# Row sums of five more blocks turned through a DMA and added on GpSimd; the last three stores on ScalarE's queue; a new order of the work

## The chip, the core and the metric

The kernel runs on one core of a Trainium2 chip. The metric is the device time of one execution in microseconds (us); the kernel before takes 324.15 us, the median of three runs (324.11 to 324.23). The profiled execution, from which all durations below are read, took 324.28 us.

## The reference

Two layers follow each other. An attention block with 32 learned queries pools each batch of 12544 rows, and its result serves as keys and values for the rows themselves; then every row goes through two products, an element-wise maximum and an output product.

```python
def mab(q, kv):                                  # scale = 1 / sqrt(128)
    s = scale * (q @ kv.transpose(0, 2, 1))
    a = np.exp(s - s.max(-1, keepdims=True))
    a /= a.sum(-1, keepdims=True) + 1e-09
    return a @ kv

h = mab(I, x)            # x (4, 12544, 128), I (4, 32, 128): h (4, 32, 128)
y = mab(x, h)            # (4, 12544, 128), taken as 50176 rows
out = np.maximum(y @ w1, y @ w2) @ w_out         # w1, w2 (128, 1024), w_out (1024, 128)
```

## The kernel before, in words

**The algebra.** y is not formed. With e2 = exp(scale x hT), a row's output is linear in e2 up to its denominator d, the sum of its 32 exponentials: out = (relu(e2 hwd) w_out + e2 m1) / d, where hwd = h (w2 - w1) and m1 = h w1 w_out. So a row needs 32 exponentials, a product of inner size 32, a relu, a product with w_out, and a scale by 1/d when the result leaves PSUM.

**Tiles.** A batch is 98 chunks of 128 rows; a block is up to four quarters of up to four chunks each, so that four products of inner size 32 run beside each other in the four row groups of TensorE. There are 28 blocks, 0 to 6 of batch 0, 7 to 13 of batch 1, 14 to 20 of batch 2, 21 to 27 of batch 3; all five that the change names are full, four chunks wide. TensorE works in three modes, and the planner charges for each switch:

- column mode: `stage` (line 637) makes a block's scores, whose exponential ScalarE writes as e2 (line 656); `pool_scores` (341) and `pool_accum` (397) pool the next batch;
- row mode: a `phase` (1093) makes four units of e2 hwd into four of the eight PSUM banks, some of them e2 m1 ("L"), and each unit's relu is taken out of PSUM by ScalarE (1119) or VectorE (1122);
- full mode: `final_one` (907) multiplies a relu chunk with w_out, eight matmuls for a chunk, up to 32 for a group, which is what is stored together. Some 14 of them stand between two phases.

**Denominators.** They are had in two ways. `dens` gives a full-mode matmul of e2 against `ones_q`, 128 by 4, for each chunk (698) and a VectorE reciprocal from PSUM (708), for a block and mostly the next one together. A block that is "turned" (21 to 27 before) does without TensorE: `den_turn` turns its e2 by a DMA transpose on SP's queue (717), `den_sum` adds the 32 columns by five GpSimd instructions (727 once, 729 four times), and `den_rp` takes the reciprocal on VectorE (736). `evict_group` multiplies a finished group by the reciprocal on VectorE (939) and stores it (969), from SP's queue or GpSimd's.

**The order.** All engines' streams are written out by a planner that runs while the program is built. It keeps a clock for TensorE, ScalarE and VectorE (class `Clock`), asks `ready` whether a piece of side work may go, decides between a phase and a final matmul by these times, and departs from its own choice where the table `DEV` says so. SP's queue has the 14 DMA transposes of x for each following batch (172), the transposes of the pooled exponentials (378) and the stores outside GpSimd's ranges; GpSimd has loads of x (166) and the other stores. The loads of a batch wait for the last `pool_accum` of the batch before it, by a copy named `pace` (164).

Of the kernel before, what the change touches and what calls it, by code (L numbers as in the profile page):

```python
# [19 lines left out]
class Clock:  # L20


    PAIR = 0.0558
# [4 lines left out]
    def __init__(self):  # L28
        self.pe = self.act = self.dve = 0.0
        self.mode = "full"  # L30
        self.bank = [0.0] * 8
        self.idle = {}
        self.log = []
        self.busy = {}
# [7 lines left out]
    def run(self, us, mode="full", ready=0.0, why="data"):  # L42
# [7 lines left out]
        return self.pe + self.LAT  # L50

# [17 lines left out]
class Block:  # L69


    def __init__(self, quarters, full=()):
# [4 lines left out]
        self.rp = None  # L77
        self.units = []
# [24 lines left out]
def kernel(  # L103
# [29 lines left out]
    rpp = ctx.enter_context(tc.tile_pool(name="rpp", bufs=5))  # L133
# [34 lines left out]
    def transpose_x_dma(b, j):  # L168
# [6 lines left out]
        st[b]["T", j] = ck.pe  # L175
# [21 lines left out]
    with tc.manual_schedule(engines={ET.PE, ET.DVE, ET.Activation, ET.Pool, ET.SP}):  # L197
# [128 lines left out]
        NEU = 5  # L326
        NU = K // U
# [7 lines left out]
        def pool_scores(b, u):  # L335
# [19 lines left out]
            ck.bank[bi] = ck.on_act(end, 0.65)  # L355
# [20 lines left out]
        def pool_turn(b, u):  # L376
            eT = etp.tile([128, 4, 128], F16, name=f"eT_{b}_{u}", tag="eT", bufs=NEU)
            nc.sync.dma_start_transpose(eT, st[b]["eu", u][0].rearrange("p (j t) -> p j t", j=4))
            st[b]["eT", u] = eT, ck.pe

        def pool_accum(b, u):
# [7 lines left out]
            if last:  # L389
                nc.vector.reduce_sum(out=acc[:, C : C + 1], in_=st[b]["es"], axis=AX.X)  # L390
                ck.on_dve(st[b]["eu", u][1], 0.1)
# [33 lines left out]
            end = ck.run(0.58 if last else 0.49, "col")  # L425
# [8 lines left out]
            if last and b + 1 < B:  # L434
                for i in range(7):
                    load_x(b + 1, i, acc[:, C : C + 1] if i == 0 else None)

# [178 lines left out]

        for n, blk in enumerate(blocks):
            blk.turned = n > 20

        def stage(blk, now=True):  # L620
# [25 lines left out]
            end = ck.run(0.054 * wd, "col")  # L646
# [36 lines left out]
        def dens(blk):  # L683
# [23 lines left out]
            end = ck.run(0.029 * n)  # L707
            nc.vector.reciprocal(out=rp[:, 0:n, :].rearrange("p t q -> p (t q)"), in_=ps[:, 0 : 4 * n])
            ck.bank[bi] = ck.on_dve(end, 0.18 + 0.001 * 4 * n)
            for blk in blks:  # L710
                blk.rpr = ck.dve + 0.2

        def den_turn(blk):
            uid[0] += 1
            eT = etp.tile([128, 4, 128], F16, name=f"den_{uid[0]}", tag="eT", bufs=NEU)[:, 0 : blk.width, :]
            e2 = blk.e2[:, 0 : 128 * blk.width]
            nc.sync.dma_start_transpose(eT, e2.rearrange("p (t k) -> p t k", k=128))
            blk.den = eT, ck.pe
            pending.append((den_sum, (blk,)))

        def den_sum(blk):
            wd = blk.width
            eT = blk.den[0].rearrange("p t (q m) -> p (t q) m", m=M)
            lo = 512 * (blk.index % 2)
# [5 lines left out]
            blk.dsum = acc[:, :, 0], ck.pe  # L730
            pending.append((den_rp, (blk,)))

        def den_rp(blk):
# [3 lines left out]
            ck.on_dve(ck.pe, 0.066 + 0.025 * wd)  # L737
# [187 lines left out]
        def evict_group(g, end):  # L925
# [39 lines left out]
            queue = nc.scalar if g is groups[-1] else nc.gpsimd if by_pool else nc.sync  # L965
            for b, c, s, m in runs:
                h = 2 if m == 4 and not by_pool and (gi in (56, 60, 64, 68, 72, 76) or 78 <= gi < 95) else m
                for lo in range(0, m, h):
                    queue.dma_start(out=outr[b, :, c + lo : c + lo + h, :], in_=osb[:, s + lo : s + lo + h, :])  # L969
# [24 lines left out]
        def want_linear():  # L994
# [113 lines left out]
        def evict_relu(q, a, u, bi, ps, end, eng=None):  # L1108
# [6 lines left out]
            ready = end + 0.03  # L1115
            if eng is None:
                eng = max(ck.act, ready) + 0.477 <= max(ck.dve, ready) + 0.597
            if eng:
                nc.scalar.activation(out=dst, in_=src, func=AF.Relu)  # L1119
                t = ck.on_act(ready, 0.477)  # L1120
            else:
                nc.vector.tensor_scalar(out=dst, in0=src, scalar1=0.0, scalar2=None, op0=ALU.max)  # L1122
                t = ck.on_dve(ready, 0.597)
# [36 lines left out]
        def ready(f, a):  # L1160

            now = ck.pe
            if f is den_turn:
                return a[0].staged <= now
            if f is den_sum:
                return a[0].den[1] + 7.5 <= now
            if f is den_rp:
                return a[0].dsum[1] + 3.0 <= now and a[0].index <= groups[min(state["g"], len(groups) - 1)].blk.index + 1
# [3 lines left out]
            if f is pool_turn and a[1] >= NEU and ("sum", a[1] - NEU) not in d:  # L1172
# [194 lines left out]
```

## Time and profile before

| what | value |
|---|---|
| median of three runs | 324.15 us (324.11 to 324.23) |
| the profiled execution | 324.28 us |
| span of its trace, first to last instruction | 322.5 us |
| TensorE busy, weight loads apart | 316.3 us, 5372 matmuls |
| VectorE busy | 280.9 us, 506 instructions |
| ScalarE busy | 281.6 us, 565 instructions |
| GpSimd busy | 63.2 us, 136 instructions |
| granted TensorE clock, mean | 0.994 |

Of the execution, 1.8 us lie outside the span. Busy time is the union of an engine's instructions. A matmul's recorded time is its latency (220 ns for the 128x128 product), while the next one may start some 56 ns later; so TensorE's pace is read from starts, and its busy share says only whether it had nothing in flight. "PE" is TensorE, "PEld" its weight loads, "DVE" VectorE, "ACT" ScalarE, "POOL" GpSimd; a q behind a name is that engine's DMA issue. Times are from the span's start.

### The profile page before, as it was taken

How to read it: one execution, taken by the hardware profiler on the slowest of the kernel's cores; microseconds unless marked ns; L12 is line 12 of the kernel's file. 1: busy time of each engine (PE TensorE's matmuls, PEld its weight loads, DVE VectorE, ACT ScalarE, POOL GpSimd, SP SyncE). 2: the span in 40 equal slices, each digit the busy share in tenths (PEclk: the TensorE clock that was granted, in tenths of full speed). 3: DMA queues.
4: the chain of work that ended last, by engine and by line, in shares of the span. 5: the costliest groups of instructions: out<-in, count | busy, mean ns of one | idle time of the engine just before them, and what ended most of it. 6: DMA issues, size and time to landing. Idle time of an engine off the chain costs nothing.

```text
span 322.5 us, 12607 instructions
## 1 busy us (share of the span) xinstructions
PE 316.3 (98%) x5372; PEld 241.3 (75%) x5372; DVE 280.9 (87%) x506; ACT 281.6 (87%) x565; POOL 63.2 (20%) x136
## 2 busy tenths in 40 slices
PE   7999999999999999999999999999999999999996
PEld 3976777777777777777777777777777777777786
DVE  3369999899979998898999998989998999899973
ACT  4779899999978999989888999988969999999960
POOL 7472012212040121221040021222006400330000
PEclk9899999999999999999999999999999999999999
DMA  8999999974289999984269999963525322442233
GB/s 206 207 263 213 218 235 233 228 152 102 100 172 241 219 234 230 239 137 128 101 124 239 232 250 226 242 133 117 118 92 109 132 83 88 120 134 95 88 116 116
DMA packets 74072, 54.12 MB, mean 168 GB/s; under 512 B 56064, under 2 KB 64032, under 8 KB 74016
## 3 DMA queue, kind: packets, MB, share of 16 engines
q1 hardware_dynamic: 64320, 27.88, 40.7%
q0 software_dynamic: 9552, 25.37, 33.5%
q8 instruction: 42, 0.69, 0.9%
q14 instruction: 14, 0.11, 0.1%
q10 hardware_dynamic: 144, 0.07, 0.1%
HBM read 27.54 MB, written 25.69 MB: 165 GB/s over the span
## 4 chain that ended last, share of the span: by engine, by line
PE 92%; DMA 5%; ACT 1%; issue 1%; POOL 0%; DVE 0%; POOLq 0%
PE ps L907 62%; PE ps L1093 23%; DMA xn<-in_x_dram 5%; PE ps L637 2%; PE ps L397 2%; PE ps L341 1%; ACT relu L1119 1%; PE ps L698 1%; PE ps L531 0%; PE ps L236 0%; PE ps L315 0%; PE ps L442 0%; PE ps L266 0%; ACT hwd L504 0%; PE ps L489 0%
## 5 line engine op out<-in xcount | busy, mean ns | idle before, releaser
L1119 ACT ACTIVATE relu<-ps 128x512 f16<-128x512 f32 x462 | 244.0, 605 | 23.6 <-PE ps L1093 16.1
L1122 DVE TENSOR_SCALAR relu<-ps 128x512 f16<-128x512 f32 x322 | 206.5, 682 | 17.7 <-PE ps L1093 15.2
L907 PE MATMUL ps<-woutp,relu 128*128 128x128 f16 x3136 | 216.9, 220 | 0.1
L907 PEld LDWEIGHTS <-relu 128*128 128x128 f16 x3136 | 176.7, 98 | 38.7 <-issue 28.2
L1093 PE MATMUL ps<-e,hwd 32*128 32x512 f16 (+2 forms) x888 | 88.9, 358 | 0.6 <-ACT hwd L504 0.6
L969 POOL DMA_DIRECT2D out_dram<-o x44 | 23.8, 542 | 148.3 <-DVE o L939 134.1
L939 DVE TENSOR_TENSOR o<-ps,rp 128x512 f32<-128x512 f32 (+3 forms) x80 | 51.2, 639 | 1.6 <-PE ps L907 1.1
L1093 PEld LDWEIGHTS <-hwd 32*128 32x128 f16 x888 | 24.9, 91 | 22.1 <-issue 0.9
L1093 PE MATMUL ps<-m,e 32*128 32x128 f16 x381 | 38.9, 217 | 0.0
L1093 PEld LDWEIGHTS <-e 32*128 32x128 f16 x381 | 21.3, 92 | 2.9 <-issue 0.4
L939 DVE TENSOR_TENSOR o<-ps,rpt 128x512 f32<-128x512 f32 (+3 forms) x28 | 17.3, 619 | 4.2 <-PE ps L884 2.2
L166 POOL DMA_DIRECT2D xn<-in_x_dram x33 | 17.9, 556 | 6.4 <-DMA xn<-in_x_dram 4.5
L247 DVE COPY xT<-ps 128x768 f16<-128x768 f16 (+6 forms) x11 | 4.8, 459 | 8.7 <-PE ps L236 8.7
L352 ACT ACTIVATE eu<-ps 128x512 f16<-128x512 f32 x18 | 10.8, 616 | 0.0
L236 PE MATMUL ps<-identity,xn 128*128 128x128 f16 x98 | 9.5, 237 | 1.2 <-DVE inducingT L786 0.6
L656 ACT ACTIVATE e<-ps 128x512 f16<-128x512 f32 (+2 forms) x21 | 10.4, 584 | 0.0
L727 POOL TENSOR_TENSOR w1T<-den 128x256 f32<-128x256 f16 (+1 forms) x7 | 4.4, 630 | 26.7 <-DMA den<-e 26.7
L729 POOL TENSOR_TENSOR w1T<-w1T 128x64 f32<-128x64 f32 (+4 forms) x28 | 8.4, 300 | 2.2
L236 PEld LDWEIGHTS <-xn 128*128 128x128 f16 x98 | 6.7, 106 | 2.8 <-DVE xn L748 0.9
L250 ACT COPY xT<-ps 128x768 f16<-128x768 f16 (+5 forms) x10 | 6.4, 670 | 2.1 <-PE ps L236 2.0
L637 PE MATMUL ps<-xT,hT 128*32 128x512 f16 (+3 forms) x118 | 8.3, 355 | 0.0
L637 PEld LDWEIGHTS <-hT 128*32 128x32 f16 x118 | 3.2, 94 | 3.8 <-issue 2.1
(95 smaller groups left out, 115.1 us busy)
## 6 DMA issues: line engine op xcount, KB each, us to landing
out_dram<-o POOLq DMA_DIRECT2D x44, 256.0 KB, 3.8
xn<-in_x_dram POOLq DMA_DIRECT2D x24, 448.0 KB, 9.7
out_dram<-o SPq DMA_DIRECT2D x28, 256.0 KB, 2.7
out_dram<-o SPq DMA_DIRECT2D x46, 128.0 KB, 1.8
wf<-in_moe_w_dram POOLq DMA_DIRECT2D x4, 256.0 KB, 5.9
xn<-in_x_dram POOLq DMA_DIRECT2D x3, 224.0 KB, 8.8
xT<-xn SPq DMA_TRANSPOSE x42, 5.5
xf<-in_x_dram SPq DMA_DIRECT2D x1, 512.0 KB, 3.7
```

The costliest lines, as they stand in the source:

```text
L166: nc.gpsimd.dma_start(out=xn_at[b, i][lo:hi, 0:n, :], in_=xr[b, lo:hi, k0 : k0 + n, :])
L236: nc.tensor.transpose(ps[:, j, :], xn_at[0, i][:, g + j, :], identity16)
L352: nc.scalar.activation(out=eu, in_=ps, func=AF.Exp, scale=scale, accum_out=st[b]["es"][:, u : u + 1])
L637: nc.tensor.matmul(out=ps[32 * q : 32 * (q + 1), 128 * t : 128 * (t + n)], lhsT=hq, rhs=xT[:, c : c + n, :], start=True, stop=True, tile_p ...
L656: nc.scalar.activation(out=blk.e2[:, lo:hi], in_=ps[:, lo:hi], func=AF.Exp, scale=st[0]["rs"] if blk.b == 0 else scale,)
L729: nc.gpsimd.tensor_add(acc[:, :, 0:n], acc[:, :, 0:n], acc[:, :, n : 2 * n])
L907: nc.tensor.matmul(out=g.ps[:, 128 * c : 128 * (c + 1)], lhsT=g.blk.relu[q][:, 128 * (jb * w4 + t) : 128 * (jb * w4 + t + 1)], rhs=woutp[: ...
L939: nc.vector.tensor_mul(osb[:, 0:n, :], g.ps[:, 0 : n * C].rearrange("p (s c) -> p s c", s=n), rp)
L969: queue.dma_start(out=outr[b, :, c + lo : c + lo + h, :], in_=osb[:, s + lo : s + lo + h, :])
L1093: nc.tensor.matmul(**seq[i])
L1119: nc.scalar.activation(out=dst, in_=src, func=AF.Relu)
L1122: nc.vector.tensor_scalar(out=dst, in0=src, scalar1=0.0, scalar2=None, op0=ALU.max)
```

## The change

1. Blocks 5, 10, 11, 12 and 19 join the turned ones: the test `n > 20` becomes membership in `TURNED`. `ready` holds a transpose back while the planner thinks that loads are under way (26.5 us from the issue of a batch's loads), or that SP's queue is far behind; `etp` has six eT buffers instead of five, `rpp` nine reciprocal buffers instead of five.
2. The planner gets clocks for SP and GpSimd, other constants for most steps, and lets `small_m1(0)` go from the second phase on.
3. The last three groups' stores are issued by ScalarE, instead of the last one alone. Which groups of 70 to 94 are stored in two halves changes.
4. `DEV` is a new table (24 entries for 28), so nearly every engine's stream after the first 29 us stands in another order.

```diff
-            blk.turned = n > 20
+        TURNED = (5, 10, 11, 12, 19, 21, 22, 23, 24, 25, 26, 27)
+            blk.turned = n in TURNED
...
+    def on_sp(self, ready, us, slow=0.0):
+        self.sp = max(self.sp, ready)
+        self.sp += slow if slow and self.sp < self.loads else us
+        return self.sp + (8.0 if self.sp < self.loads else 4.0)
...
-        st[b]["T", j] = ck.pe
+        st[b]["T", j] = max(ck.pe, ck.on_sp(ck.pe, 1.75, 4.0) - 7.0)
...
+                ck.loads = ck.pe + 26.5
...
-            blk.den = eT, ck.pe
+            blk.den = eT, ck.on_sp(ck.pe, 1.3)
...
-            lo = 512 * (blk.index % 2)
+            lo = 512 * (turned.index(blk) % 2)
...
-            queue = nc.scalar if g is groups[-1] else nc.gpsimd if by_pool else nc.sync
+            queue = nc.scalar if g in groups[-3:] else nc.gpsimd if by_pool else nc.sync
...
-            ready = end + 0.03
+            ready, ready_v = end - 0.005, end + 0.03
...
-                eng = max(ck.act, ready) + 0.477 <= max(ck.dve, ready) + 0.597
+                eng = max(ck.act, ready) + 0.487 <= max(ck.dve, ready_v) + 0.601
...
             if f is den_turn:
-                return a[0].staged <= now
+                if len(eTs) > NEU and not eTs[-NEU - 1]():
+                    return False
+                n = len(turned)
+                return a[0].staged <= now and ck.loads <= now and ck.sp <= now + (8.0 if a[0].b == 2 else 0.8) and (n < 3 or turned[n - 3].dsum is not None)
             if f is den_sum:
-                return a[0].den[1] + 7.5 <= now
+                n = turned.index(a[0])
+                return a[0].den[1] + 3.0 <= now and ck.pool <= now and (n < 2 or turned[n - 2].rp is not None)
```

Counted over the whole streams, TensorE has 20 matmuls of 128x4 and their 20 weight loads fewer (76 before, 56 now), and every other kind as often as before. TensorE changes between its modes as often as before: 222 stretches of row mode, 25 of column mode, 226 of full mode in both. Relu units move from VectorE to ScalarE, 11 of them; VectorE has two reciprocals from PSUM fewer (11, now 9) and five from SBUF more; SP issues five transposes more, GpSimd 25 additions more.

**First place: TensorE at the denominators of block 5**, whose e2 is e_216 before. The four matmuls with e_216 and two with e_252 (block 6) stand between two groups of final matmuls (ps_2078, then ps_2160):

```order
L698 MATMUL ps_2184<-ones_q,e_216_1572 128x4
L698 LDWEIGHTS e_216_1572
L698 MATMUL ps_2184<-ones_q,e_216_1572 128x4
L698 LDWEIGHTS e_252_1797
L698 MATMUL ps_2184<-ones_q,e_252_1797 128x4
L698 LDWEIGHTS e_252_1797
L698 MATMUL ps_2184<-ones_q,e_252_1797 128x4
L907 LDWEIGHTS relu_1777
L907 MATMUL ps_2160<-woutp,relu_1777 128x128
L907 LDWEIGHTS relu_1777
L907 MATMUL ps_2160<-woutp,relu_1777 128x128
```

Now the final matmuls of block 5's first group (ps_2214; line 907 is line 924 here) follow those of the group before it directly:

```order
L924 LDWEIGHTS relu_1719
L924 MATMUL ps_2030<-woutp,relu_1719 128x128
L924 LDWEIGHTS relu_1719
L924 MATMUL ps_2030<-woutp,relu_1719 128x128
L924 LDWEIGHTS relu_1788
L924 MATMUL ps_2214<-woutp,relu_1788 128x128
L924 LDWEIGHTS relu_1788
L924 MATMUL ps_2214<-woutp,relu_1788 128x128
```

Block 5's matmuls are gone; those of block 6 stand with block 7's, one group later.

**Second place: SP's queue while batch 2 is turned.** xT_94 is the turned x of batch 2, eT_0 to eT_5 its turned pooled exponentials. Before:

```order
L172 DMA_TRANSPOSE xT_94<-xn_87 128x7x128 x2
L172 DMA_TRANSPOSE xT_94<-xn_88 128x7x128 x2
L378 DMA_TRANSPOSE eT_0_3174<-eu_0_3130 128x4x128
L172 DMA_TRANSPOSE xT_94<-xn_89 128x7x128 x2
L172 DMA_TRANSPOSE xT_94<-xn_90 128x7x128
L378 DMA_TRANSPOSE eT_1_3361<-eu_1_3312 128x4x128
L172 DMA_TRANSPOSE xT_94<-xn_90 128x7x128
L378 DMA_TRANSPOSE eT_2_3487<-eu_2_3441 128x4x128
L378 DMA_TRANSPOSE eT_3_3517<-eu_3_3455 128x4x128
L378 DMA_TRANSPOSE eT_4_3802<-eu_4_3764 128x4x128
L378 DMA_TRANSPOSE eT_5_3831<-eu_5_3771 128x4x128
```

Now (line 172 is 179, 378 is 387, 717 is 731; the den tiles are those of blocks 10, 11 and 12):

```order
L179 DMA_TRANSPOSE xT_94<-xn_87 128x7x128 x2
L731 DMA_TRANSPOSE den_3122<-e_332_2341 128x4x128
L179 DMA_TRANSPOSE xT_94<-xn_88 128x7x128 x2
L387 DMA_TRANSPOSE eT_0_3201<-eu_0_3160 128x4x128
L179 DMA_TRANSPOSE xT_94<-xn_89 128x7x128
L387 DMA_TRANSPOSE eT_1_3255<-eu_1_3188 128x4x128
L179 DMA_TRANSPOSE xT_94<-xn_89 128x7x128
L179 DMA_TRANSPOSE xT_94<-xn_90 128x7x128 x2
L731 DMA_TRANSPOSE den_3488<-e_477_3167 128x4x128
L387 DMA_TRANSPOSE eT_2_3510<-eu_2_3467 128x4x128
L387 DMA_TRANSPOSE eT_3_3522<-eu_3_3474 128x4x128
L731 DMA_TRANSPOSE den_3593<-e_479_3174 128x4x128
```

Block 10's transpose stands ahead of the last six of x, those of blocks 11 and 12 behind them, among those of the pooled exponentials.

**Third place: ScalarE's last rows.** Before, four relus and the last store:

```order
L1119 ACTIVATE relu_7754<-ps_8018 128x512
L1119 ACTIVATE relu_7908<-ps_8020 128x512
L1119 ACTIVATE relu_7754<-ps_8051 128x512
L1119 ACTIVATE relu_7908<-ps_8053 128x512
L969 DMA out_dram<-o_8186 128x128
```

Now the last relus and three stores, of which the first two were SP's last two:

```order
L1139 ACTIVATE relu_7847<-ps_8110 128x4x128
L1139 ACTIVATE relu_8018<-ps_8112 128x512
L990 DMA out_dram<-o_8173 128x384
L990 DMA out_dram<-o_8195 128x256
L990 DMA out_dram<-o_8208 128x128
```

49 lines of the change are left out of this document (31 added, 18 removed), and 7 rows, old and new, of the table DEV.

## The prediction

> **What bounds the kernel now.** I read the busy time by stages first, since a mean over the span hides which stage has room. The columns are the stretch, its length, and each engine's busy us with its instructions:
>
> ```profile
> 21.00:29.00 8.00, 7.31 (x103) 4.31 (x101) 7.21 (x17) 7.58 (x18) 4.21 (x7) 1.00 1.22 205
> 29.00:100.00 71.00, 71.00 (x1226) 53.29 (x1223) 64.40 (x114) 65.73 (x134) 10.97 (x21) 1.00 0.89 184
> 100.00:200.00 100.00, 99.98 (x1681) 75.68 (x1679) 92.81 (x162) 91.67 (x185) 15.83 (x30) 1.00 0.95 197
> 200.00:300.00 100.00, 100.00 (x1688) 76.37 (x1685) 92.90 (x163) 91.70 (x182) 18.68 (x48) 1.00 0.47 123
> ```
>
> From 29 us on TensorE has something in flight all the time: 71.00 of 71, 99.98 of 100, 100.00 of 100. VectorE and ScalarE stand at 92 to 93%, with some 8 us of room in 100, and GpSimd is nearly free. Then the list of waits of TensorE alone (us in total, times, longest), of which these are the longest four:
>
> ```profile
> PE ps L753 <- DVE warm L217: 1.2, 1, 1.2
> PE ps L236 <- DVE inducingT L786: 0.6, 1, 0.6
> PE ps L1093 <- ACT hwd L504: 0.6, 1, 0.6
> PE ps L236 <- DVE xn L748: 0.4, 1, 0.4
> ```
>
> All belong to the start, the third at 24.2 us. "In flight" can still hide a small wait, so I looked at the starts where a phase stands between final matmuls, and found this as the worst after 29 us (start, length, line, count):
>
> ```profile
> 84.39 0.50 PE L907 MATMUL ps<-woutp,relu 128*128 128x128 f16 x6
> 84.81 0.51 PE L1093 MATMUL ps<-e,hwd 32*128 32x256 f16 x5
> 85.26 0.51 PE L907 MATMUL ps<-woutp,relu 128*128 128x128 f16 x6
> ...
> 152.62 0.78 PE L907 MATMUL ps<-woutp,relu 128*128 128x128 f16 x11
> 153.33 0.39 PE L1093 MATMUL ps<-e,hwd 32*128 32x512 f16 x4
> 153.65 0.90 PE L907 MATMUL ps<-woutp,relu 128*128 128x128 f16 x13
> ```
>
> At 152.62 eleven final matmuls take 0.78 us with the last one's latency of 0.22, so one starts 0.056 us after another; the last starts at 153.18, and the first after the phase at 153.65: a phase costs 0.47 us. At 84.39 six finals start, the last at 84.67, and the next one at 85.26: 0.59 us, so the phase between them waited for 0.12 us. Reading every phase that way, eight are longer than usual by 0.02 us or more, 0.3 us in all. So **the kernel is bound by what TensorE issues**, and after 29 us only about 0.3 us of its time is waiting. What the change can take away is issue time and these 0.3 us; what it can add is waits.
>
> **The change part by part.** *The matmuls that go.* Here are the ones of two blocks before, with the groups of the same line:
>
> ```profile
> 152.07 0.51 PE L907 MATMUL ps<-woutp,relu 128*128 128x128 f16 x6
> 152.42 0.34 PE L698 MATMUL ps<-ones_q,e 128*128 128x4 f16 x8
> ...
> L698 PE MATMUL ps<-ones_q,e 128*128 128x4 f16 x76 | 3.5, 165 | 0.0
> L698 PEld LDWEIGHTS <-e 128*128 128x128 f16 x76 | 3.1, 96 | 0.2 <-issue 0.2
> ```
>
> Eight start at 152.42 and the next final matmul at 152.62 (row above): 0.20 us, 25 ns each. The group's mean of 165 ns is latency that overlaps, and its weight loads of 96 ns overlap too, since eight of them pass in those 0.20 us. Bounds for one matmul: 25 ns by the starts, 96 ns if the loads came one after another. I take 25, since it is the step that the path shows. 20 x 25 ns = **-0.50 us**. They sit in full mode between final matmuls, so no mode switch goes with them, and by the two streams the numbers of switches, phases, final matmuls and all others are equal: these terms cancel. The stream up to 29 us is the same, so the start's waits stay.
>
> The Trainium skill, page "TensorE: Matmul & The Clock Gate", section "LDWEIGHTS (loading the stationary operand)", prices a load by its columns, at columns/1.2 ns: 107 ns for 128. By that price 20 loads in series would be -2.1 us. The 96 ns of the row agree with the price for one load, and the starts 25 ns apart disagree with its being paid in series.
>
> *What takes their place.* For each of the five blocks a transpose on SP, five additions on GpSimd, a reciprocal on VectorE:
>
> ```profile
> L717 SPq DMA_TRANSPOSE den<-e x7: 1191/1217/1994, 242.5 to 280.0; - x7
> ...
> L727 POOL TENSOR_TENSOR w1T<-den x7: 423/664/667, 245.0 to 283.6; 128x256 f32<-128x256 f16 x6, 128x128 f32<-128x128 f16 x1
> ...
> L729 POOL TENSOR_TENSOR w1T<-w1T x28: 205/248/457, 245.8 to 285.6; 128x64 f32<-128x64 f32 x7, 128x32 f32<-128x32 f32 x7, 128x16 f32<-128x16 f32 x7, 128x128 f32<-128x128 f32 x6
> ...
> L736 DVE RECIPROCAL rpt<-w1T x7: 194/243/245, 253.8 to 305.1; 128x16 f32<-128x16 f32 x6, 128x8 f32<-128x8 f32 x1
> ...
> L708 DVE RECIPROCAL rp<-ps x11: 249/347/349, 28.5 to 240.6; 128x32 f32<-128x32 f32 x7, 128x20 f32<-128x20 f32 x2, 128x16 f32<-128x16 f32 x1, 128x24 f32<-128x24 f32 x1
> ```
>
> SP gets 5 x 1.2 = 6.1 us. GpSimd gets 5 x (0.66 + 4 x 0.3) = 9 us, on an engine that is busy 10.97 us of 71 and 15.83 of 100. VectorE gets 5 x 0.24 and loses 2 x 0.35: +0.5 us. None of it lies on TensorE's path, and the cover is time: between a block's reciprocal and the first product that uses it the stream of VectorE has other groups' products, three for block 5, two, one and four for blocks 10 to 12. If the cover went, VectorE would stand at the reciprocal with its relus behind it, and TensorE for their banks; one turn of such a chain is a transpose's landing plus the sums, some 3.5 + 2.2 us.
>
> *The relus that move.* Eleven units go from VectorE to ScalarE:
>
> ```profile
> L1119 ACT ACTIVATE relu<-ps 128x512 f16<-128x512 f32 x462 | 244.0, 605 | 23.6 <-PE ps L1093 16.1
> L1122 DVE TENSOR_SCALAR relu<-ps 128x512 f16<-128x512 f32 x322 | 206.5, 682 | 17.7 <-PE ps L1093 15.2
> ```
>
> ScalarE +11 x 0.605 = 6.7 us (281.6 to 288), VectorE -11 x 0.682 = -7.5 us (281 to 274). Both have more idle time in the rows above than that, so nothing on the path: 0, with bounds of -0.3 us (every wait after 29 us goes) and +0.7 us (one relu late once, its row's 682 ns). I take 0, near the row of 0.12 us as the worst wait so far.
>
> *The last stores.* The end of the program, by VectorE and the queues:
>
> ```profile
> 319.16 0.79 DVE L939 TENSOR_TENSOR o<-ps,rpt 128x256 f32<-128x256 f32 x2 [0.45 <-PE ps L884]
> ...
> 318.74 1.20 SPq L969 DMA_DIRECT2D out_dram<-o  x2
> ...
> 319.99 0.37 ACTq L969 DMA_DIRECT2D out_dram<-o  x1
> ```
>
> The last product ends at 319.95 and its store goes at 319.99. With the two stores ahead on the same queue, the second must be off by then: it went at about 319.61 and takes 0.37 on ScalarE, so it is off at 319.98. The last store is late by 0 to 0.04 us; bounds 0 and +0.37 (a whole issue). I take 0. ScalarE has no relu behind these stores.
>
> **The sum** against the profiled execution: 324.28 - 0.50 + 0 + 0 = 323.78 us. The median of the runs stands 0.13 us below that execution, so 323.65; I give **323.6 us**, -0.16%. A measurement of this kernel can tell about 0.2% from no change, so faster means under 323.50 and slower over 324.80.
>
> **The rivals.** *A, the sum above*, with waits after 29 us between 0 and 0.7 us, as now 0.3: 323.3 to 324.0. *B, the new order also takes the waits away*: -0.50 - 0.3, 323.35, and to 323.0 if a few hundredths of each switch go as well. For it: the units go to the less loaded of two engines. Against it: only 0.3 us are there to be had. *C, the gain is given back at the relus*: ScalarE takes on 6.7 us and TensorE waits for banks, a few tenths at a time. Where four relus of 0.605 us on ScalarE follow an exponential, four or five late banks of 0.12 us (the row at 84.81) make up for 0.50: 324.0 to 324.8. For it stand the 92% of both engines.
>
> *D, slower: SP's queue makes the x of batch 2 late.* In the second place of the change block 10's transpose stands ahead of six transposes of x. SP is without a pause there:
>
> ```profile
> 111.66 14.57 SPq L172 DMA_TRANSPOSE xT<-xn  x8
> 126.76 1.37 SPq L378 DMA_TRANSPOSE eT<-eu  x1
> ...
> 135.42 1.78 SPq L172 DMA_TRANSPOSE xT<-xn  x1
> ...
> DMA to landing us min/median/max: 3.0/5.5/10.6
> ...
> 145.77 0.66 PE L341 MATMUL ps<-xT,inducingT 128*32 128x512 f16 x8
> ```
>
> The last x goes at 135.42 and by the median has landed at 140.9; the scores that need it start at 145.77, with 4.9 us to spare. The added transpose takes 1.2 to 2.0 of them. At the median 2.9 us are left, so nothing happens; with the longest landing, 10.6 us, x is there at 148.0, and TensorE stands 2.2 us at the scores, with everything behind it: 323.6 + 2.2 = 325.8. It decides from a landing of 7.5 us on, and is slower by over 0.2% from 8.7 on. The same holds for block 19 in batch 3. Against it: the median, and that the planner now counts SP's time.
>
> *E, the weight loads count in series* after all: 20 x 96 ns = -1.9 us, 322.2. Against it stands 152.42 to 152.62. (The page cited above would give this.)
>
> That the matmuls don't go is no rival: the streams show 56 for 76.
>
> **How the numbers follow.** A 0.58, B 0.17, C 0.13, D 0.09, E 0.03. Predicted is A's 323.6 us. The range, 322.9 to 324.8 us, takes in A, B and C with the bounds of the unknown waits, and leaves out D and E, 0.12. Of A some 0.22 lies under 323.50: faster 0.22 + 0.17 + 0.03 = 0.42, same 0.36 + 0.13 = 0.49, slower 0.09.
>
> **What would show it.** In the profile after: line 710 (the matmuls of 698) with 56 in the group and final matmuls starting 0.056 us apart where block 5's stood; TensorE busy all through the same stretches; the list of TensorE's waits with none after 29 us; ScalarE's busy time up by 6 to 7 us and VectorE's down as much; the last store some 0.5 us earlier, with about 2.5 us behind it as now. The prediction is wrong if a wait of TensorE on a DMA or on a relu shows in the middle (C, D), if the time before the first phase or behind the last store moves, or if the starts around `dens` are not 25 ns apart.

## The result, and the profile after

| | before | after |
|---|---|---|
| median of 22 runs each, on the same chip | 324.19 us (324.04 to 325.03) | 324.88 us (324.13 to 325.22) |
| the profiled execution | 324.28 us | 324.33 us |
| span of its trace | 322.5 us | 322.6 us |
| TensorE's last matmul starts | 319.40 us | 318.93 us |
| from there to the span's end | 3.10 us | 3.63 us |

After takes 1.0019 of before, 95% interval [1.0013, 1.0025]: 0.7 us more where 0.5 less was forecast. The median lies just above the range that was given (324.8 us).

The stages of after, with the columns of before (length; TensorE, its loads, VectorE, ScalarE, GpSimd; clock):

```profile
29.00:100.00 71.00, 71.00 (x1224) 53.19 (x1222) 65.39 (x116) 65.80 (x136) 12.88 (x26) 1.00 0.95 198
100.00:200.00 100.00, 100.00 (x1676) 75.74 (x1674) 90.38 (x157) 94.04 (x190) 21.66 (x45) 1.00 0.92 193
200.00:300.00 100.00, 100.00 (x1685) 76.60 (x1683) 91.33 (x162) 93.23 (x188) 20.66 (x53) 1.00 0.45 125
```

TensorE is as full as before. Its list of waits in after has the start alone, as before. Behind one for `warm` stand loads of x and hwd at 24 us:

```profile
PE ps L243 <- DMA xn<-in_x_dram: 1.1, 2, 0.9
PE ps L1113 <- ACT hwd L515: 0.6, 1, 0.6
```

The groups that the change moves, in after:

```profile
L1139 ACT ACTIVATE relu<-ps 128x512 f16<-128x512 f32 x473 | 247.8, 607 | 21.0 <-PE ps L1113 16.3 <-ACT relu L1139 0.8
L1142 DVE TENSOR_SCALAR relu<-ps 128x512 f16<-128x512 f32 x311 | 202.0, 684 | 19.1 <-PE ps L1113 16.8 <-issue 0.2
...
L710 PE MATMUL ps<-ones_q,e 128*128 128x4 f16 x56 | 2.7, 165 | 0.0
```

The 20 matmuls are gone. So the middle does what was forecast, and the place to read is the end. First TensorE's last matmul, before and after:

```profile
319.40 0.22 PE L884 MATMUL ps<-m1bd,e 128*128 128x128 f16 x1
```

```profile
318.93 0.22 PE L901 MATMUL ps<-m1bd,e 128*128 128x128 f16 x1
```

0.48 us earlier, 0.08 of it from the start (the first final matmul is at 25.71 instead of 25.79). Then what the DMA engines do from 315 to 324 us: packets, MB and share for a queue, then the last stores with their size and the median time from issue to landing. Before:

```profile
q8 instruction: 1, 0.02, 0.7%
issues: line engine op xcount, KB each, median us to landing
out_dram<-o SPq DMA_DIRECT2D x2, 128.0 KB, 1.7
out_dram<-o SPq DMA_DIRECT2D x1, 256.0 KB, 2.3
out_dram<-o SPq DMA_DIRECT2D x1, 192.0 KB, 1.8
out_dram<-o ACTq DMA_DIRECT2D x1, 64.0 KB, 1.6
```

and after:

```profile
q8 instruction: 1, 0.02, 1.0%
issues: line engine op xcount, KB each, median us to landing
out_dram<-o SPq DMA_DIRECT2D x1, 256.0 KB, 3.8
out_dram<-o ACTq DMA_DIRECT2D x1, 192.0 KB, 2.9
out_dram<-o ACTq DMA_DIRECT2D x1, 128.0 KB, 2.3
out_dram<-o ACTq DMA_DIRECT2D x1, 64.0 KB, 2.0
```

The four last stores have the same sizes, and each takes longer to land: 3.8 us for 2.3, 2.9 for 1.8, 2.3 for 1.7, 2.0 for 1.6. The last products on VectorE and the three issues on ScalarE's queue, in after:

```profile
318.68 0.80 DVE L956 TENSOR_TENSOR o<-ps,rpt 128x256 f32<-128x256 f32 x2 [0.45 <-PE ps L901]
```

```profile
318.26 1.78 ACTq L990 DMA_DIRECT2D out_dram<-o  x3
```

The last product ends at 319.48 and its store is issued at 319.66, 0.18 us after its data is there (before: 0.03). It lands 0.4 us more slowly, at 321.64 us instead of 321.57; the span ends 0.92 to 0.93 us behind that landing in both. That is where the 0.48 us went.

The row `q8 instruction` is the clue. In the packed trace it is a single packet of 16384 bytes in this window (the trace doesn't name its DMA engine): it runs from 317.21 to 318.15 us before, and from 317.92 to 319.37 us after. Of the 16 parts of a store, 15 land together in after, and the sixteenth alone is late:

| landing of the 15th and the 16th part, us | 256 KB | 192 KB | 128 KB | 64 KB, the last |
|---|---|---|---|---|
| before | 319.34, 319.63 | 320.53, 320.56 | 321.25, 321.30 | 321.54, 321.57 |
| after | 318.87, 320.68 | 320.14, 321.17 | 320.91, 321.47 | 321.27, 321.64 |

The Trainium skill, page "DMA: Bandwidth & Descriptors", section "Why a DMA increments its semaphore by 16 and not by 1", says that each DMA engine that takes part adds its own 1 behind its own data and that only the full 16 means landed. The trace agrees, with 15 at 318.87 us and the sixteenth 1.81 us later.

The whole program has 42 such packets, 0.69 MB. Between the starts of two, TensorE starts 126 matmuls by the median, so with their loads some 252 rows (a row is here one instruction of TensorE, a matmul or a weight load). **Theory F**: these packets are fetches of TensorE's instructions, some 252 at a time. A fetch comes at nearly the same count of rows each time: the last one begins at row 10665 of 10744 before, and at row 10667 of 10704 after. The change takes 40 rows off the stream (20 matmuls, 20 loads), so some 20 matmuls fewer stand behind the last fetch: it begins 1.0 us ahead of the last matmul with 19 to come, instead of 2.2 us with 40. By the theory its packet holds one DMA engine, and the last stores wait for that engine's part. The Trainium skill, page "Runtime: NRT & Kernel Launch", section "Instruction fetch mechanics", has blocks of 16 KiB, 256 instructions, which each engine's sequencer fetches through a DMA queue of its own, and calls the cost mostly hidden. The size agrees with the trace. "Mostly hidden" agrees with the middle of after, where no phase on TensorE waits longer than 0.08 us, and by theory F not with its end.

**The rivals.** S: the three stores on ScalarE's queue, which make the last one wait for two issues. W: what differs between the first profile (324.33) and the median (324.88) lies ahead of the last matmul, in waits that the profiled execution did not meet. Below, "the end" is the time from the start of the last matmul to the end of the span.

### The profile page after: what moved, and what is told of

Same layout as the page of the kernel before. It is cut to its first block, busy times and chain, and to the rows that moved or that the text cites. A ratio compares the mean times of both kernels' runs of the same rounds, so it can differ in the third digit from the quotient of the medians.

```text
span 322.6 us, 12608 instructions
## 1 busy us (share of the span) xinstructions
PE 315.3 (98%) x5352; PEld 240.1 (74%) x5352; DVE 276.6 (86%) x498; ACT 285.6 (89%) x576; POOL 73.2 (23%) x161
## 4 chain that ended last, share of the span: by engine, by line
PE 92%; DMA 5%; ACT 1%; issue 1%; POOL 0%; DVE 0%; POOLq 0%
PE ps L924 62%; PE ps L1113 23%; DMA xn<-in_x_dram 5%; PE ps L649 2%; PE ps L407 2%; PE ps L349 1%; ACT relu L1139 1%; PE ps L542 0%; PE ps L710 0%; PE ps L243 0%; PE ps L453 0%; PE ps L322 0%; PE ps L273 0%; ACT hwd L515 0%; PE ps L901 0%
## 5 line engine op out<-in xcount | busy, mean ns | idle before, releaser
L1139 ACT ACTIVATE relu<-ps 128x512 f16<-128x512 f32 x473 | 247.8, 607 | 21.0 <-PE ps L1113 16.3
L1142 DVE TENSOR_SCALAR relu<-ps 128x512 f16<-128x512 f32 x311 | 202.0, 684 | 19.1 <-PE ps L1113 16.8
L956 DVE TENSOR_TENSOR o<-ps,rp 128x512 f32<-128x512 f32 (+3 forms) x60 | 37.5, 626 | 1.7 <-PE ps L924 1.5
L956 DVE TENSOR_TENSOR o<-ps,rpt 128x512 f32<-128x512 f32 (+3 forms) x48 | 30.9, 644 | 5.4 <-PE ps L924 3.6
L745 POOL TENSOR_TENSOR w1T<-w1T 128x64 f32<-128x64 f32 (+4 forms) x48 | 14.6, 304 | 3.8
L743 POOL TENSOR_TENSOR w1T<-den 128x256 f32<-128x256 f16 (+1 forms) x12 | 7.8, 649 | 31.3 <-DMA den<-e 16.9
L243 PE MATMUL ps<-identity,xn 128*128 128x128 f16 x98 | 8.7, 220 | 1.4 <-DMA xn<-in_x_dram 1.1
L243 PEld LDWEIGHTS <-xn 128*128 128x128 f16 x98 | 6.0, 97 | 3.2 <-DMA xn<-in_x_dram 1.6
```

Of the source, the lines that this page charges most:

```text
L243: nc.tensor.transpose(ps[:, j, :], xn_at[0, i][:, g + j, :], identity16)
L745: nc.gpsimd.tensor_add(acc[:, :, 0:n], acc[:, :, 0:n], acc[:, :, n : 2 * n])
L956: nc.vector.tensor_mul(osb[:, 0:n, :], g.ps[:, 0 : n * C].rearrange("p (s c) -> p s c", s=n), rp)
```

## The experiments

Each kernel was timed against the kernel before on the same chip. The runs e5 to e8, e9 to e11 and e13 to e16 fell on chips where runs of one kernel lay further apart (the kernel before took 324.0 to 328.9 us there, median 325.4 to 325.5, and in the profiles the first final matmul comes between 25.6 and 27.7 us). So there I read the profiled execution by stages, and the medians say little.

**e1: the kernel after, unchanged.**

> The changed kernel once more, for a second profile, since its profiled execution (324.33 us) lies near the low end of its runs (324.13 to 325.22, median 324.88). Theory F (the end of the program: the last 16 KB fetch of TensorE's instructions now falls among the last stores and keeps one of the DMA engines from them, and ScalarE issues three stores one after another): the last matmul again starts 0.4 to 0.6 us earlier than in the kernel before (319.4), and what a slower execution has more lies behind it, 3.7 to 4.2 us instead of 3.1. Theory W (new waits in the middle): in a slower execution the last matmul starts at 319.4 or later. Time 324.9 by both.

324.98 us, ratio 1.0015 [1.0002, 1.0028]; the profiled execution, 325.09 us, is near the median now. ScalarE's issues and the landings at its end:

```profile
318.46 2.27 ACTq L990 DMA_DIRECT2D out_dram<-o  x3
```

```profile
q8 instruction: 1, 0.02, 1.1%
...
out_dram<-o ACTq DMA_DIRECT2D x1, 192.0 KB, 3.4
out_dram<-o ACTq DMA_DIRECT2D x1, 128.0 KB, 2.8
out_dram<-o ACTq DMA_DIRECT2D x1, 64.0 KB, 2.0
```

From the first final matmul to the last matmul it takes 293.22 us, as the first profile (293.22) and against 293.62 before. Of the 0.67 us by which this span is longer than the first, 0.47 lie at the end, which is 4.10 us now, 0.19 ahead of the first final matmul, and none between: W falls but for that start. The fetch took 1.70 us here instead of 1.45, the three issues 2.27 us instead of 1.78, and the last store went 0.66 us after its data.

**e2: one store on ScalarE's queue, as before the change.**

```diff
-            queue = nc.scalar if g in groups[-3:] else nc.gpsimd if by_pool else nc.sync
+            queue = nc.scalar if g is groups[-1] else nc.gpsimd if by_pool else nc.sync
```

> The changed kernel with its last store alone on ScalarE's queue again, the two before it on SP's; nothing else moves. Theory S (the three stores on one queue are the whole loss): about 0.6 us less than the changed kernel, 324.2 or lower. Theory F: only the late issue of the last store goes, some 0.15 us (it went 0.18 us after its data in the changed kernel's profile, 0.03 before), and one DMA engine is still late: 324.7. Theory W: no change, 324.9.

325.14 us, 1.0017 [1.0004, 1.0030]. The end is 4.10 us, as in e1. The last store goes in time and takes longer to land all the same:

```profile
319.68 0.38 ACTq L990 DMA_DIRECT2D out_dram<-o  x1
```

```profile
out_dram<-o ACTq DMA_DIRECT2D x1, 64.0 KB, 2.2
```

What lands last here, at 322.22 us, is the store before it, now on SP's queue: its issue took 0.84 us, where the other stores of SP took 0.33 at the end. The same store's took 0.90 on ScalarE's queue in e1. The queue makes no difference to the end, and the small gain that F had allowed for it did not come.

**e3: the kernel before with its last three stores on ScalarE's queue**, the reverse of e2's edit.

> The kernel before with its last three stores on ScalarE's queue; nothing else moves, and its last fetch of instructions stays where it was, 2.2 us before the last matmul. Theory S: +0.5 to 0.6 us, 324.7. Theory F: +0.15 us, 324.35. Theory W: 324.2.

324.36 us, 0.9997 [0.9984, 1.0009]:

```profile
318.93 1.69 ACTq L969 DMA_DIRECT2D out_dram<-o  x3
```

```profile
out_dram<-o ACTq DMA_DIRECT2D x1, 192.0 KB, 1.9
out_dram<-o ACTq DMA_DIRECT2D x1, 128.0 KB, 1.7
out_dram<-o ACTq DMA_DIRECT2D x1, 64.0 KB, 1.6
```

Three issues in 1.69 us, the usual landings, 3.17 us at the end: the third edit costs 0.06 us. S falls.

**e4: 40 rows added to the kernel after at its very start** (29 warming matmuls of 160 columns for 9 of 512), so that the last fetch is where it was before.

```diff
-    WARM = 9
+    WARM = 29
-            nc.tensor.matmul(out=ps, lhsT=warm[:, 0:128], rhs=warm, start=True, stop=True)
+            nc.tensor.matmul(out=ps[:, 0:160], lhsT=warm[:, 0:128], rhs=warm[:, 0:160], start=True, stop=True)
```

> The changed kernel with 29 warm-up matmuls of 160 columns instead of 9 of 512 at the start: about the same time there, and 40 instructions more ahead of all else, so that the last 16 KB fetch of TensorE's instructions comes 40 instructions earlier in the work, where the kernel before had it. The output is the same. Theory F: the late DMA engine at the end goes, 0.4 us or more less than the changed kernel, 324.0 to 324.5. Theories S and W: no change, 324.9.

325.82 us, 1.0033 [1.0016, 1.0050]: slower, though the end is 3.18 us as F says. The start lost what the end won, and more:

```profile
21.30 0.22 PE L305 MATMUL ps<-ones,et 128*128 128x1 f16 x2 [0.56 <-issue]
...
27.63 0.39 PE L924 MATMUL ps<-woutp,relu 128*128 128x128 f16 x2
```

TensorE stood 0.56 us for nothing that the profile shows, and then its granted clock fell. Here are two stretches, the clock being the third number from the end:

```profile
20.40:21.40 1.00, 0.44 (x16) 0.34 (x13) 0.85 (x2) 0.00 (x0) 0.56 (x2) 1.00 1.16 240
22.00:29.00 7.00, 6.64 (x68) 3.76 (x67) 5.37 (x11) 5.81 (x13) 3.55 (x6) 0.51 1.18 209
```

The clock stays at 0.51 until 29 us, and the first final matmul comes at 27.63 instead of 25.71. Of the twelve executions the two with a mean granted clock of 1.000 took 324.52 and 324.55 us, and the six with 0.988 or 0.989 took 326.1 to 326.4. What the 0.56 us was stays open: the packets of queue 8 nearest to it ran from 19.01 to 19.97 us and from 25.05 us, so none was under way in it.

**e5: 20 of the remaining `dens` matmuls made twice in the kernel after**, the second time into PSUM columns that nobody reads, from 36 us on.

```diff
+    spare = [20]
...
+                    for _ in range(1 if blk.index else 0):
+                        if spare[0]:
+                            spare[0] -= 1
+                            nc.tensor.matmul(out=ps[:, 256 + 4 * (n + t) : 260 + 4 * (n + t)], ...)
```

> The changed kernel with the first 20 of its remaining denominator matmuls (from 36 us on) made twice, the second time into columns that nobody reads: 40 instructions of TensorE more, ahead of the last fetch but behind the start, which stays as it is. Theory F (the place of the last 16 KB fetch of instructions makes the loss): the last matmul starts 0.5 us later than in the changed kernel (319.1 in its second profile, so 319.6), and 3.1 to 3.2 us follow it instead of 4.1: 324.4 to 324.5, less than the changed kernel though it does more. Rival N (the tail has another cause): the tail stays at 4.1 and the time is 325.4.

The profiled execution takes 324.56 us. The last matmul is at 319.51 us, 293.65 us behind the first final one (0.43 more than in after), and the end is 3.18 us. Putting 20 matmuls in costs what taking 20 away had brought, and the end is as before the change. So this one edit undoes both effects of the change, the shorter middle and the longer end. (Median 325.53 us, 0.9995 [0.9979, 1.0010].)

**e6: 108 such doubles in the kernel before**, 216 rows, so that its stream ends at the same distance from a fetch as that of after.

> The kernel before with 108 denominator matmuls repeated in the same way: 216 instructions more, so that, counted in 256, its last fetch falls where the changed kernel has it, some 27 instructions from the end. No part of the change is in it. Theory F: 108 x 25.6 ns = 2.8 us more up to the last matmul (322.2) and a tail of 3.6 to 4.1 us instead of 3.1: 327.5 to 327.9. Rival N: tail 3.1, 327.0.

328.68 us, 1.0087 [1.0059, 1.0114]. The program has 43 fetches, one more, and the end is 4.16 us:

```profile
q8 instruction: 43, 0.70, 1.0%
```

```profile
out_dram<-o ACTq DMA_DIRECT2D x1, 64.0 KB, 2.3
```

Nothing of the change is in this kernel, and it has the end of the kernel after.

**e7: the kernel before with the new set of turned blocks alone**, under its own planner.

```diff
-            blk.turned = n > 20
+            blk.turned = n in (5, 10, 11, 12, 19, 21, 22, 23, 24, 25, 26, 27)
```

> The kernel before with the five blocks turned and nothing else of the change: its table, its planner, its queues for the last stores. It has as many instructions of TensorE as the changed kernel. Theory F: last matmul at 318.9 to 319.1 (0.5 us less, if the added transposes make no new waits), tail 3.6 to 4.1 us: 324.5 to 324.9. Rival N: the tail is the changed kernel's order's or queues', so 3.1 us here, 323.7.

327.19 us, 1.0053 [1.0031, 1.0076]. The end is 4.17 us, with after's count of rows. But TensorE also waits in the middle, which after does not. SP's queue and TensorE:

```profile
98.11 5.13 SPq L969 DMA_DIRECT2D out_dram<-o  x3
103.33 5.92 SPq L172 DMA_TRANSPOSE xT<-xn  x1
```

```profile
113.46 0.38 PE L1093 MATMUL ps<-m,e 32*128 32x128 f16 x4 [0.91 <-DVE o L939]
```

Three stores take SP 5 us and a single transpose 6, and a product on VectorE (line 939) is late, with TensorE's banks behind it: 1.28 us in all at this phase. The product starts at 112.72 us. The first of the three stores, which left at 98.11, landed only at 112.62, and it holds the output buffer that this product needs: there are six (`outp`), and it is the sixth product behind that store's. So it waited for a store, and not for a reciprocal or for x as in the prediction's rival D. In after no phase waits longer than 0.08 us.

**e8 and e11: 40 rows added to the kernel after where TensorE waits anyway**: 20 small transposes behind those of w1h, in the 0.56 us that it stands for hwd, written beside them in one bank.

```diff
+            for _ in range(20 if g else 0):
+                nc.tensor.transpose(ps[:, 4, 0:32], w1h[0:32, 0:128], identity16[0:32, 0:32])
```

> The changed kernel with 20 transposes of 32 columns more, behind the second weight transpose at 23.1 us, where TensorE waits 0.56 us for ScalarE's hwd anyway; the output is the same. 40 instructions more at no cost, if the wait hides them. Theory F: last matmul at 319.1, tail 3.1 to 3.2: 324.0, below the kernel before (324.2). Rival N: 324.9.

> The same kernel as the one with 20 small transposes added at 23 us, where TensorE waits for hwd (40 rows more, 10733). There TensorE had lost 1.4 us ahead of the added rows, at loads of x, so its time said little. Theory F: the end is 3.1 to 3.2 us again, the added rows cost nothing where they stand, and with the start of the kernel after the time is about 323.9 us, 0.9 us under the kernel after and 0.3 under the kernel before. If the added rows are what made that start late, the first final matmul comes 1 us or more later again, and the time is 325 us or more.

Both have the end of 3.16 to 3.17 us, and neither the expected total: 325.48 us, 0.9991 [0.9976, 1.0006], and 325.29 us, 0.9994 [0.9978, 1.0011]. In e8's profile TensorE waited longer for the loads of x, ahead of the added rows (1.8 us, in after 1.1). In e11's the copy `w1T` waits for the added transposes of its bank, and the first final matmul comes 3.63 us behind the first phase instead of 3.20 to 3.27 in the four profiles of after. So the place was not free.

**e9 and e10, repeated as e15 and e16: fewer rows still.** In the kernel after, 16 of the 3136 final matmuls are left out, 32 rows, so that the stream ends ahead of the last fetch; and, as a control, 4 of them, so that it does not.

```diff
+        left = [16]
...
+            if jb == 3 and g.blk.b == 1 and left[0]:
+                left[0] -= 1
+            else:
```

> The kernel after, with 16 of its 3136 final matmuls left out (one of the eight of each chunk of four groups of batch 1, so those rows of the output lack a part): 32 rows fewer on TensorE, 10661. Theory F (the last fetch of TensorE's instructions, at about row 10665, falls among the last stores): the stream now ends ahead of the point where that fetch begins, so it does not come at all. The last matmul comes 0.9 us earlier (16 x 56 ns), and the time from it to the end of the span falls to 3.0 to 3.2 us: about 323.2 us, some 1.5 us under the kernel after and faster than the kernel before. If the longer end has another cause, it stays at 3.6 to 4.1 us and only the 0.9 us come: 324.0.

> The control to the run with 16 left out: only 4 of the final matmuls are left out (of one group, so its rows lack a part), 8 rows fewer, 10685. Theory F: the fetch still comes, now some 19 rows ahead of the end, so the end stays at 3.6 to 4.2 us, or grows by 0.1 to 0.2 us since the fetch starts later; only 4 x 56 ns = 0.2 us go: about 324.7 to 324.9 us. If leaving matmuls out takes the longer end away by itself, 3.1 us at the end and about 323.8.

> The kernel with 16 of the final matmuls left out (four groups of batch 1 lack a part), again. Theory F: the last fetch does not come, 3.1 to 3.2 us at the end, and a median 1.7 to 1.9 us under the kernel after of this job (0.9 from the matmuls, 0.5 to 1.0 from the end), about 323.2 us. If only the matmuls count: 0.9 us under it, 324.0.

> The control with 4 left out (one group lacks a part), again. Theory F: the fetch still comes among the last stores, the end is 3.6 to 4.2 us, and the median is 0.2 to 0.6 us under the kernel after of this job. If leaving matmuls out shortens the end by itself: 3.1 us and 1.1 us under it.

In e9 the 42nd fetch does not come, and in e15 it comes 1.9 us behind the end of the span. Of e9:

```profile
q8 instruction: 41, 0.67, 0.9%
```

```profile
out_dram<-o ACTq DMA_DIRECT2D x1, 64.0 KB, 1.6
```

The end is 3.16 and 3.17 us, and all 16 parts of each of the last four stores land together again: in e9 the sixteenth comes 0.03 to 0.04 us behind the fifteenth. In the control e10, whose last fetch stands 7 matmuls ahead of the end, the end is 3.61 us. There the last store lands in the usual 1.6 us, but goes 0.54 us after its data, since the issue of the store before it takes 0.78 us instead of 0.34. The end goes as F says. The total does not: of the 0.9 us that 16 matmuls issue, 0.2 came (293.02 us from the first final matmul to the last, against 293.22). The phases of batch 1 around them grew by 0.7 us together, which may be since less time between phases leaves less for the relus (not tried). One of them in e9, and the same one in after:

```profile
110.38 0.39 PE L1117 MATMUL ps<-e,hwd 32*128 32x512 f16 x3
110.64 0.38 PE L1117 MATMUL ps<-m,e 32*128 32x128 f16 x4
```

```profile
110.69 0.39 PE L1113 MATMUL ps<-e,hwd 32*128 32x512 f16 x3
110.70 0.39 PE L1113 MATMUL ps<-m,e 32*128 32x128 f16 x4
```

In e9 the phase's fourth unit starts 0.26 us behind the others, in after 0.01. The medians: e9 325.15 us, 1.0000 [0.9980, 1.0019], e10 325.45 us, 1.0007 [0.9989, 1.0024]; e15 324.90 us, 0.9968 [0.9940, 0.9996], e16 325.46 us, 0.9986 [0.9959, 1.0012]. They stand in the order that F gives, and 0.3 and 0.6 us apart. e10's profile has 294.40 us from the first final matmul to the last, 1.2 more than after: TensorE waits there for transposed x of batch 3, 0.44 us in the longest wait at 199.9 us. This is the wait that rival D feared, but ahead of block 19's transpose on SP (212.4 us), so without D's cause. (The profiled execution of e16 took 540 us, with final matmuls 0.106 us apart by the mean instead of 0.057, so its end is not compared.)

**e12: the same 20 transposes in columns of their own.**

```diff
+            if g:
+                i = min(range(8), key=lambda j: ck.bank[j])
+                pad = psum.tile([128, 32], F16, name="pad", tag=f"bank{i}", bufs=1)
+                for _ in range(20):
+                    nc.tensor.transpose(pad, w1h[0:32, 0:128], identity16[0:32, 0:32])
```

> The kernel after with 20 small transposes added in TensorE's wait for hwd at 23 us, as before, but into PSUM columns of their own, which nobody reads, so that the copy w1T does not wait for them. Theory F: the added 40 rows put the last fetch 67 rows ahead of the end, the end is 3.1 to 3.2 us, the first final matmul stands 3.3 us behind the first phase as in the kernel after, the last matmul comes where it came there (318.9 to 319.1 with an equal start), and the time is 323.9 to 324.1 us, under the kernel after by 0.8 and under the kernel before by 0.1 to 0.3 where the starts are equal. If the added rows cost time where they stand, the first final matmul is 0.5 us later behind the first phase, and the time is 324.4.

324.36 us (324.13 to 324.60), 1.0001 [0.9992, 1.0010], and 3.18 us at the end. The bank that is free first was the one whose copy had just been asked for:

```profile
24.19 0.60 PE L585 MATMUL pad<-identity,w1h 32*128 32x32 f16 x18 [0.52 <-DVE w1T L588]
```

The transposes waited for it, and the first final matmul came 3.60 us behind the first phase. The end is mended, the place again not free.

**e14 and e18: the same in another bank**, with the kernel after beside them as e13 and e17.

```diff
-                i = min(range(8), key=lambda j: ck.bank[j])
+                i = min((j for j in range(8) if j != bi), key=lambda j: ck.bank[j])
```

> The kernel after, unchanged, as the partner of the other three runs of this job: 324.9 to 325.0 us with 4.1 us (3.6 in a lucky execution) from the last matmul to the end of the span, if the chip lets the start go as it did in the first runs.

> The kernel after with the 20 small transposes at 23 us in a PSUM bank that is not the one of the copy w1T (in the run before, the bank was the same one, and the transposes waited 0.52 us for that copy). Theory F: 3.1 to 3.2 us at the end, the first final matmul 3.3 us behind the first phase as in the kernel after, so 0.9 us under the kernel after: 324.0 us, and 0.2 under the kernel before. If the rows cost time wherever they stand, 324.4 as in the run before.

> The kernel after, unchanged, as the partner: 324.9 to 325.0 us where the start holds still, 3.6 to 4.2 us at the end.

> The kernel after with 20 small transposes at 23 us in a PSUM bank of their own, again. Theory F: 3.1 to 3.2 us at the end, and a median 0.9 us under the kernel after of this job, 0.2 under the kernel before: 324.0 us where the start holds still.

On the quiet chip of e17 and e18: after 325.06 us (324.64 to 325.23), 1.0020 [1.0011, 1.0030]; the padded kernel **324.19 us** (324.02 to 324.64), 0.9996 [0.9987, 1.0005]. On the other chip after took 325.75 us, 1.0006 [0.9984, 1.0028], and the padded kernel 325.23 us, 0.9979 [0.9956, 1.0001]. In e18 the added rows cost nothing, as the first and second phase show (23.11 is the transposes' row of w1h, and 24.14 the phase that waits for hwd, 24.08 in after):

```profile
23.11 0.39 PE L580 MATMUL ps<-identity,w1h 128*128 128x128 f16 x4
23.43 0.66 PE L585 MATMUL pad<-identity,w1h 32*128 32x32 f16 x20
24.14 0.40 PE L1118 MATMUL ps<-e,hwd 32*128 32x128 f16 x10
```

and the last store is back at its old landing, while that of e17 (below it) is not:

```profile
out_dram<-o ACTq DMA_DIRECT2D x1, 64.0 KB, 1.6
```

```profile
out_dram<-o ACTq DMA_DIRECT2D x1, 64.0 KB, 2.0
```

Twenty matmuls more, 0.87 us less in the median. In the profiles the span is 0.90 us shorter: 0.69 of it is the end (3.16 us for 3.85), and 0.21 the start.

All profiled ends, from the packets of queue 8 and the matmuls' starts:

| kernel | last fetch begins, us ahead of the last matmul | matmuls behind it | it takes, us | end, us |
|---|---|---|---|---|
| e9; e15 | 7.0 (the one before); none in the span | 127; none | 1.4; none | 3.16; 3.17 |
| before | 2.2 | 40 | 0.9 | 3.10 |
| e14, e18 | 2.2, 2.1 | 39, 38 | 1.1, 1.3 | 3.16, 3.16 |
| e4, e5, e8, e11 | 2.0 | 36 to 37 | 1.1 to 1.4 | 3.16 to 3.18 |
| e3, e12 | 1.75 | 32 | 0.9 | 3.17, 3.18 |
| after, e1, e13, e17 | 1.0 to 1.1 | 18 to 20 | 1.45, 1.70, 1.84, 1.53 | 3.63, 4.10, 4.14, 3.85 |
| e2, e6, e7 | 1.0 | 19 | 1.57 to 1.71 | 4.10 to 4.17 |
| e10 | 0.3 | 7 | 0.96 | 3.61 |

Nineteen profiles fall in two groups. With 32 matmuls or more behind the last fetch, or no fetch there at all, the end is 3.10 to 3.18 us; with 7 to 20 it is 3.6 to 4.2. The kernel, the queue of the stores and the kind of rows added or taken don't decide it. Counted in rows, the 42nd fetch begins at row 10665 to 10683 in every one of them whose stream is longer than that; that of e9 and e15 ends at row 10672.

The stores tell the groups apart as well. In the eight profiles with the longer end the sixteenth part of the 192 KB store comes 0.72 to 1.54 us behind the fifteenth, and the issue of the last store but one takes 0.43 to 0.92 us. In the other eleven it is 0.02 to 0.05 us, and 0.33 to 0.34 us. So it is shown in both directions that the place of the last fetch makes the longer end. That the packet and the late part share a DMA engine is inferred from the times, and how a fetch makes an issue longer is not shown.

## Why the prediction was wrong, step by step

- **"20 x 25 ns = -0.50 us": right, and 0.39 measured.** From the first final matmul to the last it is 293.62 us in two profiles of before's stream (before, e3) and 293.22 to 293.23 in seven of after's (after, e1, e2, e13, e14, e17, e18): -0.39 us, and e5 puts it back (293.65). Read phase by phase as in the prediction, waits of TensorE after 29 us are 0.6 us instead of 0.3, none longer than 0.08 us, where 0.12 was the worst: that is 0.3 us given back. In e5 the stretches of `dens` are 0.50 us longer for 20 doubles, so the 25 ns hold. By these numbers some 0.2 us more went elsewhere in the stream; where was not traced.
- **"What takes their place": nothing on the path, right.** GpSimd has 10.0 us more (9 forecast). Rival D did not come in after. SP's last transposes of x for batch 2, in after:

```profile
128.40 5.53 SPq L179 DMA_TRANSPOSE xT<-xn  x3
```

  They end at 133.9 us, where the last one before started at 135.42: the new order sends them earlier.
- **"The relus that move": 0 taken, inside its bounds; the size of the shift was too large.** The 0.3 us of new waits of the point above stand at phases; what they wait for was not traced. ScalarE's busy time rose by 4.0 us (6.7 forecast), VectorE's fell by 4.3 (7 forecast): the group's mean of 0.605 us overlaps with the next relu, and its busy time per relu is 244.0 / 462 = 0.53 us. That would still be 5.8 us for 11 relus; where the rest went was not traced.
- **"The last stores ... I take 0": this step failed, with "about 2.5 us behind it as now".** By itself the move to ScalarE's queue costs 0.06 us (e3), inside the bounds. But the step took the rest of the end for granted. It asked when each store is issued, and not when it lands, and had no term for TensorE's fetches, which move when its rows get fewer. The last store's landing grew by 0.4 us and its issue came up to 0.6 us later, since the change itself moved TensorE's last fetch among the stores. The end grew by 0.53 us in the first profile, and by 0.75 to 1.04 in the three others. Against -0.39 that gives the slower median: between e1 and e3, on one chip, the middle is -0.40 us, the end +0.93 and the first final matmul -0.07, together +0.46 of 0.56 between their profiled executions (325.09 and 324.53), and 0.62 between their medians.
- **The rivals.** None named this. E fell with the first point, and B did not come. Of C at most the 0.3 us of new waits came, and the middle kept its gain. "Slower" had 0.09, all of it on D, and the end had no rival of its own, though the prediction listed it among what would make it wrong. D's own bounds hold a slip: with 2.9 us left at the landing of 5.5 us it decides from 8.4 us on, and not from 7.5, and is slower by over 0.2% from 9.6 on, and not from 8.7.

With the fetch out of the end (e14, e18) the change is worth what its own terms give, within the measurement: -0.35 us of span in e18's profile against before's first, and in the medians 0.9996 and 0.9979 of before, neither interval clear of 1. A version that is certainly faster than before was not found.

## What to carry to other kernels

What is taken out of an instruction stream moves what goes by the stream's position, here the instruction fetches; so after a change of some tens of rows, look for the `instruction` packets of the DMA queues and at what stands beside the last ones. At a kernel's end read stores by their landing and not by their issue alone; here a store was done when its slowest sixteenth was. Where a fetch falls into the end, a few idle instructions in a wait that exists anyway can move it out (e18: 0.87 us), but only in a bank of their own and after a look at who waits for whom there.

## What the runs showed of the hardware that had not been expected

- TensorE's instructions come in packets of 16384 bytes, one for some 252 of its matmuls and loads, and the last ones take 0.9 to 1.8 us each. 216 rows more made one packet more (e6), 32 rows fewer one fewer within the span (e9, e15).
- A store's last part comes late beside such a packet: in after 15 parts of one had landed at 318.87 us, and the last came at 320.68. Without the packet (e9) the same store's last part came 0.04 us behind the others.
- The issue of a store can stretch as well: three of them took 1.69 us in e3, 1.78 in after and 2.27 in e1. So can the landing: a store of e7 that left at 98.11 us landed at 112.62.
- A pause of TensorE of 0.56 us at 20.7 us was followed by a granted clock of 0.51 from 22 to 29 us (e4); the pause for hwd before 24.2 us in the kernel before, as long, left it at 1.00 (the row from 21 to 29 us in the prediction). Why the two differ is not shown.
